# Batch 1's feed-forward work in units of 256 tokens, batch 2's casts later, and second layers held back in batch 0

## The chip, the cores and the metric

The kernel runs on one core of one Trainium2 chip. A core has five engines with queues of their own, each worked in order: TensorE for matrix products (PE in the profile, its weight loads PEld), VectorE (DVE), ScalarE (ACT), GpSimd (POOL) and SyncE (SP), which here issues most of the DMAs. Engines wait for each other by semaphores. Matrix products are written to PSUM, of which this kernel uses eight banks, and copied from there by ACT or DVE. The metric is the device time of one execution in microseconds (us).

## The reference

Two layers, one after the other. The first is causal attention in a sliding window with a bias that falls with distance (batch 8, 8 heads, 576 tokens, head size 64):

```
scores = scale * q @ k.T                       # window of 128, causal
scores = where(0 <= i - j < 128, scores - slope[h] * |i - j|, -1e9)
x = softmax(scores) @ v                        # 4608 tokens x 512 (heads side by side)
```

The second sends every token through eight experts (512 to 1024 to 512), weighted by a matrix P that is normalised over rows and columns eight times:

```
P = exp(x @ w_gate - max);  8 times: rows to sum 1, columns to sum 1, times N/E
out = sum over e of P[:, e] * (relu(x @ w1[e]) @ w2[e])
```

## The kernel before

The program order is written out by hand; each engine runs its instructions in that order. It has three stages: attention, with the products of experts 0 and 1 put between its steps as filling for PE; the normalisation of P, filled in the same way; and experts 2 to 7 with fewer and smaller products. The change lies in the first stage.

Attention goes through 8 batches. A batch of 576 tokens has five key blocks (four of 128, a tail of 64), and every block two halves of four heads: ten half-blocks, counted by `at = 2 * kb + u`. A half-block has scores on PE (`scores`, L372, into `psS`, a pair of two-bank buffers), the exponential on ACT (`exps`, L390), the masking product on DVE (`masks`, L403) and the product with the values on PE (`values`, L426, into `psN`). DVE divides by the row sums (L436, L437, into `xsb`). `turn_x` turns a block of the result: for batches 0, 1, 2 and 7 by PE into `psX` with a copy to `xT` (L457, L465), else by a transposing DMA (L467). `xT` is the input of the experts.

Before a batch's scores, q and k are loaded (`load_qk`, L232, on SP), cast to half precision four times two heads at a time (`cast_qk`: k by ACT at L247, q by DVE at L245, into `c16`), and turned. For batches 0 to 2 `turn_pe` turns them on PE into `psT` (L311); ACT copies the k side to `kN` (L326), DVE the q side to `qN` (L324), and the tail of 64 goes with `j = NDT` through ACT into `tT` (L320). From batch 3 on `turn_qk` issues two transposing DMAs (L261), and `order_qk` copies their result on POOL and DVE (L272). The load of v (L334), its cast on POOL (L344), `load_tail` (L223) and the stores of finished second layers (`store`, L487) are also issued from inside the loop; SP takes all its DMAs in the order written.

`Filler` holds the work of experts 0 and 1 as units of an expert and a span of token blocks of 128. A unit has eight chains of first-layer products (`l1`, L102: four matmuls into one bank `psh`, then a relu on ACT to `hT`, L109) and one second-layer chain for each block (`l2`, L115: eight matmuls into `psy`, then a copy on DVE to `yo`, L499, or to `y_first`, L495). `take` gives the next chain. It starts a unit when no first-layer chain is left and at most two second-layer chains are, takes a second-layer chain after two first-layer ones, and reckons 0.87 us for a first-layer chain of 512 columns and 1.74 us for a second-layer one. `start_unit` takes the first unit in the list whose blocks are written (`ready`) and whose expert is `allowed`; expert 1 is allowed from half-block 4 of batch 1 on. Each half-block takes its share of what is ready: what is left in the list divided by the half-blocks left.

The units are spans of blocks (0, 1), (2, 3), then four blocks each: (4 to 7), (8 to 11) and on. Blocks 0 to 3 are batch 0, 4 to 7 batch 1. Scores, filling, turns, gates and value products share four PSUM banks under the tag `pmm`: all but the scores, which have `psS`.

The loop over half-blocks writes out, in order: budget, the next half-blocks' scores and exponential, 1 us of filling, masks, values, the turn of the finished block, the rest of the filling, and then the loads and casts that are due at this half-block.

Of the kernel before, what the change touches and what calls it, by code (L numbers as in the profile page):

```python
# [14 lines left out]
def kernel(  # L15
# [25 lines left out]
    NG = Ntok // GT  # L41
# [105 lines left out]
    class Filler:  # L147


        def __init__(self, units):  # L150
            self.todo = list(units)
            self.l1: list = []
            self.l2: list = []
            self.l1_us = 0.0
            self.since = 0
            self.ready = 0
            self.allowed = {0}

        def start_unit(self):
            for n, (e, b0, nb, make) in enumerate(self.todo):  # L160
                if b0 + nb <= self.ready and e in self.allowed:
                    self.todo.pop(n)
                    self.l1_us = L1_US * nb / 4
                    self.l1, self.next_l2 = make()
                    return True
            return False

        def take(self):
            if not self.l1 and len(self.l2) <= 2:
                if self.start_unit():  # L170
                    self.since = 0
            use_l2 = bool(self.l2) and (not self.l1 or self.since >= 2)
            if use_l2:
                self.l2.pop(0)()
                self.since = 0
                cost = L2_US
            elif self.l1:
                self.l1.pop(0)()
                self.since += 1
                cost = self.l1_us  # L180
                if not self.l1:
                    self.l2 = self.l2 + self.next_l2
            else:
                return 0.0
            return cost
# [17 lines left out]
    if True:  # L203
# [33 lines left out]
        def cast_qk(b, j):  # L237

            if j == 0:
                c16s[b] = per.tile([P, 2, RI, H, Dh], FP16, name=f"c16_{b}", tag="a8", bufs=8)  # L240
            for n in (1, 0):
                src = raw[b][n][:, 2 * j : 2 * j + 2, :].rearrange("p h (i d) -> p i h d", i=RI)
                to = c16s[b][:, n, :, 2 * j : 2 * j + 2, :]
                if n == 0:
                    nc.vector.tensor_copy(out=to, in_=src)  # L245
                else:
                    nc.scalar.copy(out=to, in_=src)  # L247
            if j == NDT - 1:
                raw.pop(b)
# [52 lines left out]
        def turn_pe(b, kq, j):  # L302

            wide = j == NDT
            ps = aps.tile([P, RI, P], FP32 if wide else FP16, name=f"psT_{b}_{kq}_{j}", tag="pmm", bufs=4)
            for i in range(RI):
                if wide:
                    src = tails[b][:, 2 * i : 2 * i + 2, :]
                else:
                    src = c16s[b][:, kq, i, 2 * j : 2 * j + 2, :]  # L310
                nc.tensor.matmul(  # L311
                    out=ps[:, i, :],
                    lhsT=src.rearrange("p h d -> p (h d)"),
                    rhs=ident32 if wide else ident,
                    is_transpose=True,
                    start=(i == 0),
                    stop=(i == RI - 1),
                )
            if wide:
                nc.scalar.copy(out=QKT[b][2], in_=ps)  # L320
                return
            to = QKT[b][kq][:, j].rearrange("p (r i) -> p r i", i=RI)
            if kq == 0:
                nc.vector.tensor_copy(out=to, in_=ps.rearrange("p i r -> p r i"))  # L324
            else:
                nc.scalar.copy(out=to, in_=ps.rearrange("p i r -> p r i"))  # L326
# [71 lines left out]
        def masks(b, kb, u):  # L398
            nk, nn = sizes(kb)
            pt = pts[b, kb, u]  # L400
            hs = slice(4 * u, 4 * u + 4)
            w = nk + nn
            nc.vector.tensor_tensor(  # L403
                out=pt[0:nk, :, 0:w], in0=pt[0:nk, :, 0:w], in1=mask[0:nk, hs, 0:w], op=ALU.mult
            )
# [38 lines left out]
        def by_pe(b):  # L444
            return b < XPE or b == B - 1
# [53 lines left out]
            nc.vector.tensor_copy(out=yo, in_=ps)  # L499
            stores.append((e, blk, yo))  # L500

        spans = [(0, 2), (2, 2)] + [(4 * g, 4) for g in range(1, NG)]
        order = [(0, 0), (0, 1)]
        for n in range(2, len(spans)):
            order += [(0, n), (1, n - 2)]
        order += [(1, len(spans) - 2), (1, len(spans) - 1)]
        filler = Filler(
            (e, *spans[n], lambda e=e, n=n: unit_atoms(e, *spans[n], aps, ("pmm", "pmm"), (4, 4), keep))
            for e, n in order
        )  # L510
# [77 lines left out]
        def some(n):  # L588
            for _ in range(min(n, len(todo))):
                todo.pop(0)()  # L590
# [36 lines left out]
        for n, (b, kb, u) in enumerate(steps):  # L627
            nxt = steps[n + 1] if n + 1 < len(steps) else None
            at = 2 * kb + u
            left = ((8 if b < XPE else 10) - at) % 10 + 1  # L630
            budget = filler.backlog() / (11 if (b, at) == (XPE, 0) else left)
            if nxt:
                if nxt[0] < XPE and nxt[1:] == (RI - 2, 1):
                    turn_pe(nxt[0], 0, NDT)
                if nxt == (1, 0, 0):
                    cast_qk(1, 0)
                    cast_qk(1, 1)
                    for j in range(NDT):
                        turn_pe(1, 1, j)
                        turn_pe(1, 0, j)  # L640
                        if j < 2:
                            cast_qk(1, j + 2)
                        filler.fill(1.0)
                if n == 0:
                    scores(*nxt)
                elif nxt[2] == 0:
                    scores(*nxt)
                    scores(*nxt[:2], 1)
                exps(*nxt)
            got = filler.fill(1.0)  # L650
            if nxt:
                masks(*nxt)
            values(b, kb, u)
            if n > 0 and u == 0 and by_pe(steps[n - 1][0]):
                turn_x(*steps[n - 1][:2])
            if u == 1 and n // 2 + NKB < B * NKB:
                cast_v(n // 2 + NKB)
            filler.fill(budget - got)
            if at == 0 and b > XPE:
                filler.ready = 4 * b  # L660
            if at < 8 and b < XPE:
                filler.ready = 4 * b + at // 2
            if at == 8 and b < XPE:
                filler.ready = 4 * b + 4
            if u == 1 and not by_pe(b):
                turn_x(b, kb)
            if u == 1:
                if kb == 1 and b > 0:
                    gates(4 * b - 4, 4 * b)
                if n // 2 + NKB + 1 < B * NKB:  # L670
                    load_v(n // 2 + NKB + 1)
            if b == 0 and at == 1:
                load_weights(1)
            if b == 1 and at == 4:
                filler.allowed.add(1)
                nc.sync.dma_start(out=ysp[0, 0:RI].rearrange("m p d -> p m d"), in_=first_y[0])
            if (b, at) == (0, 3):
                load_qk(2)
            if (b, at) == (0, 7):
                homes(1)  # L680
            if (b, at) == (1, 3):
                homes(2)
            if b == 1 and 3 <= at <= 6:
                cast_qk(2, at - 3)
            if b == 1 and 4 <= at <= 7:
                turn_pe(2, 1, at - 4)
                turn_pe(2, 0, at - 4)
            if 1 <= b < B - 2 and at == 3:
                load_qk(b + 2)
            if 1 <= b < B - 2 and at >= 8:  # L690
                cast_qk(b + 2, at - 8)
            if 2 <= b < B - 1:
                if at < 2:
                    cast_qk(b + 1, at + 2)
                if at == 1:
                    turn_qk(b + 1)
                    order_qk(b + 1, 1, range(NDT))
                if at == 5:
                    turn_tail(b + 1)
                if at in (6, 7):  # L700
                    order_qk(b + 1, 0, range(2 * at - 12, 2 * at - 10))
            if b < B - 1 and at == (1 if b > 1 else 5) and b:
                load_tail(b + 1)
            if 10 * b + at >= 66:
                i = 10 * b + at - 66
                if i % 8 == 0:
                    home_last(2 + i // 8)
                (load_w2 if i % 8 < 4 else load_w1)(2 + i // 8, i % 4, 4)
            if (b, at) == (7, 0):
                todo += sums_of(2, *extras(2))  # L710
            if b == 7 and at >= 5:
                some(1)
# [270 lines left out]
        for n in range(N):  # L983
            g = units[n - 1][0]
# [62 lines left out]
```

## Time and profile before

| | |
|---|---|
| median of 3 runs | 1061.02 us (1057.84 to 1062.36) |
| the profiled execution | 1060.31 us, its span 1058.5 us |
| PE busy | 1031.1 us, 97% of the span |
| DVE, ACT, POOL busy | 631.7, 434.5, 77.4 us |
| PE busy in the stretch 0 to 27 us | 17.09 us |
| in 27 to 58 us | 22.19 of 31 us |
| in 58 to 78 us | 19.40 of 20 us |
| in 78 to 113 us | 34.57 of 35 us |

All times within the profile are counted from the span's start. A row of the timeline gives start, length, engine, line, operation, what it writes and reads, and how many instructions in a row are taken together; in brackets, how long the engine stood idle before and what released it. Batch 1's scores begin at 42 us, batch 2's at 76.74, batch 3's at 112.85. An engine's length of one instruction holds a latency that overlaps the next one, so that starts are closer together than lengths.

### The profile page before, as it was taken

What the parts mean: (1) busy time and instruction counts of PE and PEld (TensorE: products, weight loads), DVE (VectorE), ACT (ScalarE), POOL (GpSimd) and SP (SyncE); (2) the same over time, 40 slices, a digit from 0 to 9 for tenths busy, and PEclk for the clock granted to TensorE, in tenths of its full rate; (3) what the DMA queues carried; (4) which work ended last, traced back from release to release, by engine and by line L of the source; (5) the groups of instructions that cost most, each with busy time, mean ns of one, the idle gap of its engine ahead of it and who ended that gap; (6) DMA issues with size and microseconds to landing.
All of it is one profiled execution on the core that took longest, in us unless ns stands there. A gap on an engine that the chain in (4) does not pass through costs nothing.

```text
span 1058.5 us, 21148 instructions
## 1 busy us (share of the span) xinstructions
PE 1031.1 (97%) x9006; PEld 802.9 (76%) x9006; DVE 631.7 (60%) x1171; ACT 434.5 (41%) x729; POOL 77.4 (7%) x139
## 2 busy tenths in 40 slices
PE   6789999999999999999999999999999999999998
PEld 4455444444544888888888888888888888888887
DVE  4655665655687665655655655655655655555555
ACT  6556555555233333333333333333333333333332
POOL 2112032325100000000000000000000000000000
PEclk9999999999999999999999999999999999999999
DMA  9985599879992501211211210211220220220240
GB/s 226 252 221 139 114 201 218 196 154 177 182 207 70 115 23 49 71 26 46 71 39 33 70 49 23 71 39 32 71 65 7 71 68 3 71 71 1 71 90 20
DMA packets 166110, 98.55 MB, mean 93 GB/s; under 512 B 84960, under 2 KB 157440, under 8 KB 166016
## 3 DMA queue, kind: packets, MB, share of 16 engines
q1 hardware_dynamic: 151280, 79.21, 29.4%
q0 software_dynamic: 14304, 17.84, 10.2%
q8 instruction: 70, 1.15, 0.4%
q14 instruction: 24, 0.20, 0.1%
q10 hardware_dynamic: 432, 0.16, 0.1%
HBM read 87.74 MB, written 19.02 MB: 101 GB/s over the span
## 4 chain that ended last, share of the span: by engine, by line
PE 92%; DMA 4%; SPq 2%; DVE 1%; ACT 1%; issue 0%; POOL 0%; ACTq 0%
PE psh L834 36%; PE psS_m L889 31%; PE psh L102 11%; PE psy L115 10%; DMA v<-in_v_dram 2%; DMA k<-in_k_dram 2%; PE psN L426 1%; PE psS L372 1%; DMA xT<-xsb 1%; SPq L334 1%; SPq L223 0%; SPq L288 0%; PE psy L954 0%; PE psG L473 0%; ACT hT L109 0%
## 5 line engine op out<-in xcount | busy, mean ns | idle before, releaser
L841 ACT ACTIVATE hs<-psh 128x512 f16<-128x512 f32 x432 | 258.0, 597 | 453.2 <-PE psh L834 373.7
L834 PE MATMUL psh<-aux,w1l 128*128 128x256 f16 x2880 | 372.6, 273 | 0.2 <-ACT hs L841 0.2
L834 PEld LDWEIGHTS <-w1l 128*128 128x128 f16 x2880 | 281.7, 98 | 33.3 <-issue 0.5
L889 PEld LDWEIGHTS <-hs 128*128 128x128 f16 x2568 | 251.3, 98 | 29.1
L846 DVE TENSOR_TENSOR hs<-hs 128x1024 f16<-128x1024 f16 x107 | 74.1, 693 | 274.5 <-ACT hs L841 274.3
L889 PE MATMUL psS_m<-w2l,hs 128*128 128x256 f16 x1440 | 186.6, 273 | 0.0
L102 PE MATMUL psh<-xT,w1t 128*128 128x512 f16 (+1 forms) x640 | 141.1, 359 | 4.4 <-DMA xT<-xsb 1.7
L115 PE MATMUL psy<-w2t,hT 128*128 128x512 f16 x576 | 133.8, 379 | 3.4 <-DMA w2t<-in_moe_w_dram 2.8
L818 DVE TENSOR_TENSOR aux<-xT,pbc 128x1024 f16<-128x1024 f16 x108 | 131.4, 1217 | 2.5 <-DMA pbc<-ptd 2.5
L109 ACT ACTIVATE hT<-psh 128x512 f16<-128x512 f32 (+1 forms) x160 | 87.6, 556 | 100.6 <-PE psh L102 99.3
L115 PEld LDWEIGHTS <-hT 128*128 128x128 f16 x576 | 53.7, 98 | 64.6 <-issue 4.8
L102 PEld LDWEIGHTS <-w1t 128*128 128x128 f16 x640 | 57.9, 99 | 53.6 <-issue 6.4
L390 ACT ACTIVATE pt<-psS 128x1024 f16<-128x1024 f32 (+2 forms) x80 | 67.5, 852 | 45.9 <-PE psS L372 37.0
L935 DVE TENSOR_TENSOR acc<-acc,psS_m 128x256 f32<-128x256 f32 (+1 forms) x162 | 74.3, 504 | 12.4 <-PE psS_m L889 11.1
L499 DVE CAST yo<-psy 128x512 f16<-128x512 f32 x68 | 46.9, 690 | 55.5 <-PE psy L115 54.3
L403 DVE TENSOR_TENSOR pt<-pt,mask 128x1024 f16<-128x1024 f16 (+2 forms) x80 | 50.2, 627 | 41.5 <-ACT pt L390 41.4
L889 PE MATMUL psS_m<-more,hs 128*128 128x256 f16 x576 | 74.6, 273 | 0.0
L834 PE MATMUL psh<-aux,w1t 128*128 128x256 f16 x576 | 74.6, 273 | 0.0
L849 DVE TENSOR_TENSOR hs<-hs 128x1024 f16<-128x1024 f16 x107 | 73.2, 684 | 0.0
L834 PEld LDWEIGHTS <-w1t 128*128 128x128 f16 x576 | 56.4, 98 | 6.5
L535 POOL DMA_DIRECT2D w2t<-in_moe_w_dram x2 | 1.8, 878 | 705.2 <-PE psS_m L889 669.8
L426 PEld LDWEIGHTS <-pt 128*128 128x128 f16 (+2 forms) x576 | 28.6, 101 | 26.1 <-DVE pt L403 6.8
(83 smaller groups left out, 657.2 us busy)
## 6 DMA issues: line engine op xcount, KB each, us to landing
pbc<-ptd SPq DMA_DIRECT2D x108, 128.0 KB, 4.5
y<-ysp SPq DMA_DIRECT2D x36, 256.0 KB, 4.7
ysp<-yo SPq DMA_DIRECT2D x68, 128.0 KB, 3.1
v<-in_v_dram SPq DMA_DIRECT2D x32, 256.0 KB, 3.9
out_dram<-acc SPq DMA_DIRECT2D x31, 256.0 KB, 2.4
q<-in_q_dram SPq DMA_DIRECT2D x7, 1024.0 KB, 6.4
k<-in_k_dram SPq DMA_DIRECT2D x7, 1024.0 KB, 9.8
w2t<-in_moe_w_dram POOLq DMA_DIRECT2D x4, 1024.0 KB, 14.7
```

Of the source, the lines that this page charges most:

```text
L102: nc.tensor.matmul(out=ps[:, 0:nt], lhsT=w1ts[e][:, dt, P * ft : P * ft + P], rhs=xT[:, b0 : b0 + nb, dt, :], start=(dt == 0), stop=(dt == ...
L109: nc.scalar.activation(out=st["hT"][:, ft, 0:nt], in_=ps[:, 0:nt], func=AF.Relu)
L115: nc.tensor.matmul(out=ps, lhsT=st["hT"][:, ft, P * ms : P * ms + P], rhs=w2ts[e][:, ft, :], start=(ft == 0), stop=(ft == NFT - 1),)
L390: nc.scalar.activation(out=pt[0:nk, :, 0 : nk + nn], in_=ps[0:nk, :, :, 0 : nk + nn].rearrange("p a y n -> p (a y) n"), func=AF.Exp, scale ...
L403: nc.vector.tensor_tensor(out=pt[0:nk, :, 0:w], in0=pt[0:nk, :, 0:w], in1=mask[0:nk, hs, 0:w], op=ALU.mult)
L818: nc.vector.tensor_tensor(out=xs(n).rearrange("p (d b t) -> p d b t", d=NDT, b=2), in0=xT[:, 2 * g : 2 * g + 2].rearrange("p b d t -> p d ...
L834: nc.tensor.matmul(out=ps[:, f, :], lhsT=W1L[e][:, dt, P * ft : P * ft + P], rhs=xs(n)[:, HB * dt : HB * dt + HB], start=(dt == 0), stop=( ...
L841: nc.scalar.activation(out=h[n][:, 2 * i : 2 * i + 2, :], in_=ps, func=AF.Relu)
L846: nc.vector.tensor_tensor(out=t[:, NFT : NFT + NF2, :], in0=a[:, 0:NF2, :], in1=a[:, NF2:NFT, :], op=ALU.add)
L849: nc.vector.tensor_tensor(out=t[:, NFT + NF2 : 2 * NFT, :].rearrange("p f n -> p (f n)").rearrange("p (f t) -> p f t", t=P), in0=a[:, :, P ...
L889: nc.tensor.matmul(out=Ms[g, bank][:, half, :], lhsT=left(n, m, f), rhs=W2L[e][RIGHT[m]][:, f, :], start=(e == 2 and f == 0 and half == 0) ...
L935: nc.vector.tensor_tensor(out=a, in0=a, in1=p2, op=op)
```

## The change

Three things are altered in the writing order of the first stage.

- The spans of batch 1 are of two blocks, like batch 0's: (4, 5) and (6, 7) take the place of (4 to 7), for expert 0 and expert 1. The order of the list stays: expert 0's span n ahead of expert 1's span n - 2.
- `Filler` has a flag `hold`, with which `take` gives no second-layer chain. It is lifted at half-block 7 of batch 0, behind that half-block's filling.
- Batch 2's casts, which stood at half-blocks 3, 4, 5 and 6 of batch 1 (two heads each, k and q), stand at 5 (two of the four), 6 and 7. Its turns on PE, at 4, 5, 6 and 7 before, stand at 6 (two of the four), 7 and 8, in each half-block ahead of the cast.

In the order that results, PE takes expert 0's unit on blocks 4 and 5 ahead of expert 1's first unit, and expert 1's unit on blocks 4 and 5 is also taken within batch 1; the units on blocks 6 and 7 fall into batch 2. From batch 3's scores on PE's order of work is as before. The lines below are moved by at most four in the changed file.

```diff
             self.allowed = {0}
+            self.hold = True
...
-            use_l2 = bool(self.l2) and (not self.l1 or self.since >= 2)
+            use_l2 = bool(self.l2) and not self.hold and (not self.l1 or self.since >= 2)
...
-        spans = [(0, 2), (2, 2)] + [(4 * g, 4) for g in range(1, NG)]
+        spans = [(2 * g, 2) for g in range(4)] + [(4 * g, 4) for g in range(2, NG)]
...
                 filler.ready = 4 * b + 4
+            if (b, at) == (0, 7):
+                filler.hold = False
...
-            if b == 1 and 3 <= at <= 6:
-                cast_qk(2, at - 3)
-            if b == 1 and 4 <= at <= 7:
-                turn_pe(2, 1, at - 4)
-                turn_pe(2, 0, at - 4)
+            if b == 1 and 5 <= at <= 8:
+                for j in ((), (0, 1), (2,), (3,))[at - 5]:
+                    turn_pe(2, 1, j)
+                    turn_pe(2, 0, j)
+                for j in ((0, 1), (2,), (3,), ())[at - 5]:
+                    cast_qk(2, j)
```

## The prediction

> **What bounds the kernel now.** I read the page's busy shares and slices first, then the list of who waited for whom on PE, then PE's and ACT's timelines over the first 160 us, then SP's. Times below are us from the span's start.
>
> ```profile
> PE 1031.1 (97%) x9006; PEld 802.9 (76%) x9006; DVE 631.7 (60%) x1171; ACT 434.5 (41%) x729; POOL 77.4 (7%) x139
> ...
> PE   6789999999999999999999999999999999999998
> ```
>
> PE is busy 97% of the span, so the end moves by what PE loses or wins idle: 27.4 us in all, 18 of them before 58 us. The waits, longest first in total:
>
> ```profile
> PE psT L311 <- ACT c L247: 7.0, 3, 5.3
> ...
> PE psX L457 <- ACT tT L320: 2.9, 1, 2.9
> PE psy L115 <- DMA w2t<-in_moe_w_dram: 2.8, 1, 2.8
> PE psh L102 <- DMA xT<-xsb: 1.7, 1, 1.7
> ...
> PE psh L102 <- ACT hT L109: 0.9, 2, 0.4
> ```
>
> The 7.0 is mostly the cold start, which the change leaves alone. The two waits it aims at are the 2.9 and the 2.8. On PE's timeline (start, length, instructions, and in brackets the idle before and its releaser):
>
> ```profile
> 30.32 1.89 PE L115 MATMUL psy<-w2t,hT 128*128 128x512 f16 x8 [2.75 <-DMA w2t<-in_moe_w_dram]
> ...
> 55.77 0.59 PE L457 MATMUL psX<-ident,xsb 128*128 128x128 f16 x4 [2.89 <-ACT tT L320]
> ...
> 57.89 1.62 PE L102 MATMUL psh<-xT,w1t 128*128 128x256 f16 x8
> ```
>
> The 2.89 is ACT's doing. The turn of block 1 of batch 1 needs the PSUM bank that held batch 1's tail, ACT empties that bank with the copy tT, and tT stands behind batch 2's first k cast, which waits for its load:
>
> ```profile
> 54.62 0.62 ACT L247 CAST c<-k 128x512 f16<-128x512 f32 x1 [2.90 <-DMA k<-in_k_dram]
> 55.14 0.58 ACT L320 CAST tT<-psT 128x512 f16<-128x512 f32 x1
> ...
> 108.94 0.60 ACT L247 CAST c<-k 128x512 f16<-128x512 f32 x1
> ...
> 147.33 0.62 ACT L247 CAST c<-k 128x512 f16<-128x512 f32 x1 [5.18 <-DMA k<-in_k_dram]
> ```
>
> The idle also costs clock. Windows of 1 us; the granted clock is the number before the last two:
>
> ```profile
> 54.00:55.00 1.00, 0.00 (x0) 0.00 (x0) 0.00 (x0) 0.39 (x1) 0.00 (x0) 1.00 1.17 196
> 56.00:57.00 1.00, 1.00 (x12) 0.94 (x9) 0.32 (x1) 1.00 (x2) 0.00 (x0) 0.50 1.21 209
> 58.00:59.00 1.00, 1.00 (x6) 0.69 (x6) 1.00 (x3) 0.50 (x1) 0.00 (x0) 0.50 0.72 120
> 60.00:61.00 1.00, 1.00 (x11) 0.90 (x10) 0.99 (x2) 0.72 (x2) 0.92 (x5) 1.00 0.81 182
> ```
>
> Half speed lasted from about 55.8 to 59.05. The 2.75 idle at 27.6 did not bring it on.
>
> **Part 1, the hold.** Expert 0's first second-layer chain moves behind one group of value products (0.24 us). It still waits for w2t, which lands at 30.3 whatever PE does, so PE resumes at 30.32 as before. It then runs the same work and stands at about 34.8 before batch 1's first k cast (ACT, 35.17, released by its load). That load covers the 0.24: no gain. If it came early, 0.24 would be won. The reordering gives the next first-layer chain another bank, one that doesn't wait for the copy kN ending at 36.86: I take 0.3, between 0 and 0.6.
>
> **Part 2, batch 2's casts later.** ACT reaches tT at 52.1 instead of 55.14. The turn then waits for xsb (DVE, done 52.98) and starts at 53.05. Scores of block 3 follow by 54.2. The first filler chain is now expert 0 on the first 256 tokens of batch 1, which needs the xT copy behind that turn. DVE has queued ahead of it mask 0.69, reciprocal 0.17, product 0.42, from ACT's exponential ending at 53.65, so xT is there at 55.3. Filler starts at 55.33 instead of 57.89: 2.56 won. The clock stays full, so the first two chains take 0.94 instead of 1.46: 0.52 won. The wait of 0.60 at 64.83 (a bank behind a relu) has no counterpart in the new order: 0.60 won. Batch 2's first eight transposes, run inside those 2.56 us before, come later: 0.45 lost. Two relu waits of 0.2 appear where six or eight 256-column chains stand in a row and ACT has two casts and an exponential between them: 0.4 lost. With part 1's 0.3 that is 3.1 won up to batch 2's scores.
>
> **Part 3, units of 256 tokens.** PE pays nothing: 8 matmuls of 256 columns and 4 of 512 both take 0.87 us start to start (59.59 to 62.21 is three times eight; 85.75 to 86.61 is four). ACT pays:
>
> ```profile
> L109 ACT ACTIVATE hT<-psh 128x512 f16<-128x512 f32 x26 | 15.3, 599 | 11.0 <-PE psh L102 11.0
> L109 ACT ACTIVATE hT<-psh 128x256 f16<-128x256 f32 x32 | 12.0, 387 | 7.9 <-PE psh L102 7.0
> ```
>
> Sixteen relus of 512 become 32 of 256: 32 x 0.387 - 16 x 0.599 = 2.8 us more on ACT, hidden while PE has other work. 13.88 us of PE work (16 chains of 0.435, 4 of 1.73) move from batch 2 into batch 1. So batch 2's scores, at 76.74 before, start at 76.74 + 13.88 - 3.1 = 87.5.
>
> Batch 2 is then short of PE cover at its start. ACT has, start to start as its timeline spaces them, kN 0.49, three casts of batch 3 (0.51 each), three exponentials (0.92 each) and a relu of 0.36 for every 0.435 us of PE work. By that queue PE idles 0.5 (the last q copy stands behind two yo casts on DVE), 1.2 and 0.4, against 0.43 before: 1.7 lost. Batch 3's scores start at 87.5 + (112.85 - 76.74 - 13.88) + 1.7 = 111.4 instead of 112.85. The gain is down to 1.45.
>
> **Part 4, what is late next.** SP works in order, and the load of batch 4's q and k stands behind the two transposing DMAs of batch 3, which wait for batch 3's last cast:
>
> ```profile
> 89.59 5.05 SPq L261 DMA_TRANSPOSE qk<-c  x2
> ...
> 99.07 1.13 SPq L232 DMA_DIRECT2D k<-in_k_dram  x1
> ```
>
> ```profile
> k<-in_k_dram SPq DMA_DIRECT2D x1, 1024.0 KB, 9.4
> ```
>
> Transposes to k issue: 9.48. Issue to landing: 9.4. In between stand the same issues after as before. In the run before, k landed at about 108.5 and ACT cast it at 108.94, with no slack to speak of. After, batch 3's last cast ends about 9.35 us behind the start of batch 2's scores (12.85 before; less filler precedes it): ACT's queue to its third exponential is 0.49 + 3 x 0.51 + 3 x 0.92 + 6 x 0.36 = 6.94 with 0.8 of waits for PE, and DVE follows with mask 0.69, reciprocal, product and q cast, 1.6. That is 96.85. So k lands at 96.85 + 18.9 = 115.75, against a step that wants it near 108.5. Behind that cast ACT has batch 3's first exponential and the relus. PE fills four banks and stands: the fourth chain of batch 3 starts at 115.75 + cast 0.5 + exponential 0.92 + relu 0.6 = 117.85 (117.13 before), after 2.2 us idle; the sixth, behind another cast and exponential, at 120.75 (119.90 before). From there the order is the old one. **Sum: +0.85, call it +0.9**: 2.56 + 0.52 + 0.60 + 0.3 - 0.45 - 0.4 - 1.7 = 1.45 won, and 2.3 taken back by the load.
>
> The profiled execution took 1060.31 (span 1058.5), 0.7 under the median of 1061.02; its sum is 1061.2, and on the median 1061.9.
>
> What the trace can't show is bounded so. The new idle of 2.2 lies between one of 1.70 (at 152.93) and one of 2.75, and the clock stayed at 1.00 behind both, so I take 0; if it acts like the 2.89, half of 3.25 us is lost at worst, 1.6. Load times of 8.6 to 10.0 in the batches behind it move the sum by 0.8 either way; 17.45, as batch 2's k needed beside the weights, is the far end.
>
> The Trainium skill, "TensorE: Matmul & The Clock Gate", section "What's actually happening", has the clock halve only after an idle window of some 3.4 us. This trace disagrees: 2.89 us were enough. By the page the new idle costs nothing (1061.9); by the row at 2.89 up to 1.6 (1063.5).
>
> **Rivals.**
> - *The load is no limit* (0.25). For it: transposes or load a little quicker, or batch 3's cast earlier, and k is there. Against it: it would have to gain 2 to 3 us on a chain whose parts all come from rows. The gain of 1.45 stays, or up to 3.1 if batch 2's ACT waits don't show: 1057.9 to 1059.6.
> - *Slower for good* (0.16). Place: the k load of batch 4, ACT's queue behind it. If it takes 17.45 like batch 2's, 8 us are added: 1070. It decides from 4.4 us of further lateness (5.3 less 0.9). For it: ACT already waited 5.18 for the same load one batch later, at 147.33. Against: DMA is idle from 80 to 88 us, the weights are long in.
> - *Faster by over 0.5%* (0.08). All 3.1 stay and the 0.25 and 1.70 waits at 150 to 153 go as well, with the 0.43: 5.5 won, 1055.5. Nothing in the order touches those two.
> - *The hold does nothing*: certain as far as w2t goes; it is in the forecast.
>
> **How the numbers follow.** The forecast (the load takes the gain back, 1060.5 to 1063.5) has 0.51. Half a percent, about what a measurement can tell from no change here, is 5.3 us. Forecast and first rival lie within it: 0.76; slower 0.16; faster 0.08. Range 1057 to 1066: the first rival's end below, the clock's 1.6 and half of what the load could add above.
>
> **What would show it.** Right: no wait of psX for tT near 53; filler from about 55.3; the clock at 1.00 from 55 to 60; batch 2's scores near 87.5; new waits of psh for relus at 91 to 97; the transposing DMAs near 97; ACT waiting some 6 to 7 us for k before 116, and PE idle some 2 us just after. Wrong, if ACT's cast at batch 3's start waits for nothing, or if that wait exceeds 11 us.

## The result, and the profile after

The changed kernel took 1064.99 us (median of 8 runs, 1063.92 to 1065.95) against 1059.70 of the kernel before in the same session (8 runs, 1056.66 to 1062.36). The ratio is 1.0045, with a 95% interval of 1.0032 to 1.0059: 0.45% slower, where 1061.9 us was forecast. The profiled execution took 1064.4 us, its span 1062.6, 4.1 more than before.

The first lines of the page of the changed kernel, its busy shares and two rows of slices:

```profile
PE 1037.3 (98%) x9070; PEld 812.1 (76%) x9070; DVE 632.8 (60%) x1171; ACT 436.5 (41%) x745; POOL 77.8 (7%) x139
...
PE   5899899999999999999999999999999999999998
...
PEclk9989999999999999999999999999999999999999
```

PE's busy time grew by 6.2 us (1031.1 before), although the products are the same. Most of that is work at a lower clock, which the third slice of the clock row shows; some 1.0 us more is busy time at full clock in batch 2 (see part 3 below). PE's timeline shows the places of the steps (start, length, instructions, idle before and its releaser):

```profile
53.16 0.59 PE L458 MATMUL psX<-ident,xsb 128*128 128x128 f16 x4 [0.23 <-ACT tT L321]
...
55.70 1.86 PE L102 MATMUL psh<-xT,w1t 128*128 128x256 f16 x8 [1.11 <-DVE xT L466]
...
115.71 0.31 PE L427 MATMUL psN<-v,pt 64*64 64x65 f16 x4 [1.36 <-DVE pt L404]
...
118.33 1.46 PE L102 MATMUL psh<-xT,w1t 128*128 128x512 f16 x4 [0.78 <-DVE xT L466]
...
125.78 1.02 PE L102 MATMUL psh<-xT,w1t 128*128 128x512 f16 x4 [0.42 <-ACT hT L109]
```

The 2.89 us wait of psX for tT is down to 0.23, and the first chain on batch 1's tokens starts at 55.70 instead of 57.89. But from there to the next start its first two chains take 1.66 us (57.36), where 0.94 was expected. The third line, a wait of the last value products for a mask on DVE, is new.

What PE waited for in batch 2 and at batch 3's start, first in the kernel before (76 to 120 us), then in the changed one (88 to 127 us); columns are the total, the number and the longest:

```profile
PE psh L102 <- ACT hT L109: 0.9, 2, 0.4
PE psh L102 <- DVE xT L465: 0.5, 1, 0.5
```

```profile
PE psh L102 <- ACT hT L109: 1.4, 2, 1.0
PE psN L427 <- DVE pt L404: 1.4, 1, 1.4
PE psh L102 <- DVE xT L466: 0.8, 1, 0.8
PE psS L373 <- ACT c L248: 0.5, 1, 0.5
PE psN L427 <- DVE xsb L438: 0.4, 1, 0.4
```

The table splits the first stage at points that all kernels have: batch 1's first scores, batch 2's, batch 3's, the sixth chain of batch 3 (after the second relu wait), and batch 7's first scores. Columns are the differences of the start times; from there to the end the order is the same in all. So that columns compare, 13.88 us of filling that the change moves from batch 2 into batch 1 are booked in batch 2 throughout (6.94 in E7 and E11, where half of it is moved). E1 to E12 are the experiments below; "half speed" lists the stretches between 40 us and the last 2 us with a granted clock of 0.50. Each row is one profiled execution, and that can lie off the median: E2's and E12's were the slowest of their runs, E5's the fastest. Two things lie outside the sum. Batch 1's first scores come at 41.1 to 42.1 us in most traces, but at 43.2 to 43.6 in E4, E9, E10 and E12. And behind batch 7's first scores all take 811.4 to 812.7 us, but E11 takes 815.1.

| kernel | batch 1 | batch 2 | to 6th chain | to batch 7 | sum | median us | half speed |
|---|---|---|---|---|---|---|---|
| before | 34.75 | 36.11 | 7.05 | 127.23 | 205.14 | 1059.70 | 55.7-59.1 |
| changed | 34.73 | 40.05 | 9.30 | 125.35 | 209.43 | 1064.99 | 50.5-60.7, 118.8-122.2 |
| E1 casts only | 32.54 | 36.78 | 7.05 | 125.27 | 201.64 | 1059.23 | 50.0-53.4 |
| E2 units only | 36.27 | 39.36 | 10.31 | 126.38 | 212.32 | 1064.18 | 49.7-53.1, 56.5-63.3, 117.9-124.8 |
| E3 old units | 32.53 | 36.78 | 7.74 | 125.48 | 202.53 | 1057.91 | 50.0-53.4 |
| E4 | 32.03 | 40.08 | 9.31 | 126.15 | 207.57 | 1064.83 | 117.6-121.0 |
| E5 early k | 31.61 | 40.43 | 10.05 | 124.89 | 206.98 | 1065.44 | 113.6-120.4 |
| E6 q on ACT | 34.69 | 39.16 | 7.94 | 124.61 | 206.40 | 1063.32 | 50.0-60.2 |
| E7 filling kept | 34.41 | 38.32 | 7.93 | 125.64 | 206.30 | 1061.97 | 50.0-60.2 |
| E8 | 32.53 | 36.79 | 7.10 | 128.35 | 204.77 | 1059.53 | 49.3-52.8 |
| E9 spare | 31.61 | 40.04 | 10.16 | 125.87 | 207.68 | 1063.92 | 116.2-119.6 |
| E10 old units, spare | 31.31 | 36.78 | 7.36 | 127.04 | 202.49 | 1056.84 | none |
| E11 kept, spare | 31.29 | 38.31 | 7.58 | 125.76 | 202.94 | 1059.09 | 356.5-359.9 |
| E12 all | 31.63 | 39.36 | 7.00 | 126.16 | 204.15 | 1058.94 | none |

The changed kernel loses nothing in batch 1 and gains nothing there either. It loses 3.9 in batch 2 and 2.25 behind it, and 1.9 comes back later, where a wait of 0.68 (137.93) of before is down to 0.25 and one of 1.70 (152.93) is gone.

### The profile page after: what moved, and what is told of

Read it like the earlier page. It is cut to its first block, busy times and chain, and to the rows that moved or that the text cites. A ratio compares the mean times of both kernels' runs of the same rounds, so it can differ in the third digit from the quotient of the medians.

```text
span 1062.6 us, 21293 instructions
## 1 busy us (share of the span) xinstructions
PE 1037.3 (98%) x9070; PEld 812.1 (76%) x9070; DVE 632.8 (60%) x1171; ACT 436.5 (41%) x745; POOL 77.8 (7%) x139
## 4 chain that ended last, share of the span: by engine, by line
PE 85%; DVE 0%; ACT 0%; issue 0%
PE psh L838 36%; PE psS_m L893 31%; PE psy L115 8%; PE psh L102 8%; PE psN L427 1%; PE psS L373 1%; PE psy L958 0%; PE psG L474 0%; DVE yo L500 0%; PE psX L458 0%; PE psC L763 0%; DVE pt L404 0%; ACT hs L845 0%; PE psP L778 0%; DVE L_sb L766 0%; PE psS L380 0%
## 5 line engine op out<-in xcount | busy, mean ns | idle before, releaser
L102 PE MATMUL psh<-xT,w1t 128*128 128x512 f16 (+1 forms) x704 | 146.1, 350 | 4.8 <-DVE xT L466 3.1
L109 ACT ACTIVATE hT<-psh 128x512 f16<-128x512 f32 (+1 forms) x176 | 89.8, 522 | 105.8 <-PE psh L102 104.2
L102 PEld LDWEIGHTS <-w1t 128*128 128x128 f16 x704 | 66.0, 101 | 52.9 <-issue 9.6
L838 PEld LDWEIGHTS <-w1t 128*128 128x128 f16 x576 | 56.4, 98 | 6.5
```

The lines of the kernel that those rows point to most:

```text
L102: nc.tensor.matmul(out=ps[:, 0:nt], lhsT=w1ts[e][:, dt, P * ft : P * ft + P], rhs=xT[:, b0 : b0 + nb, dt, :], start=(dt == 0), stop=(dt == ...
L109: nc.scalar.activation(out=st["hT"][:, ft, 0:nt], in_=ps[:, 0:nt], func=AF.Relu)
L838: nc.tensor.matmul(out=ps[:, f, :], lhsT=W1L[e][:, dt, P * ft : P * ft + P], rhs=xs(n)[:, HB * dt : HB * dt + HB], start=(dt == 0), stop=( ...
```

## The experiments

Two theories stood at first. CLOCK: the changed kernel's batch 1 runs at half speed for 10 us, and that costs the time. COVER: the filling that left batch 2 hid ACT's and DVE's queues and the load of batch 4's k, and these now show. Each session had its own runs of the kernel before: 1059.23 us for E1 to E4 (23 runs), 1059.22 for E5 to E8 (25) and 1059.64 for E9 to E12 (29).

**E1, the casts alone** (kernel before, only the block of batch 2's casts and turns changed).

```diff
-            if b == 1 and 3 <= at <= 6:
-                cast_qk(2, at - 3)
...
+            if b == 1 and 5 <= at <= 8:
```

> The kernel before with the third part alone: batch 2's casts and turns at the later half-blocks, units and second layers as before. Theory COVER (the loss comes from filling that left batch 2, so that its ACT and DVE queues and the load of batch 4's k show): no filling moves here, so the stall of 2.9 us behind tT goes and little is given back: 2 to 3 us faster than before, a ratio of 0.997 to 0.998, and ACT's first cast of batch 4 waits less than 1 us. Theory CLOCK (the loss comes from PE's clock being halved from about 50.4 to 60.4 us in the changed kernel, against 55.8 to 59.05 before): the half-speed stretch starts near 50 here as well, and the ratio is 1.000 to 1.003.

1059.23 us (12 runs), ratio 0.9998 [0.9986, 1.0009]. The profiled execution is 3.5 shorter up to batch 7; the median moved by nothing. The ratio lies between the two theories' ranges. The runs lie between 1056.5 and 1062.0, so a gain of some 2 us can't be told here. The casts are not what costs.

**E2, the units alone** (kernel before, only the spans changed).

```diff
-        spans = [(0, 2), (2, 2)] + [(4 * g, 4) for g in range(1, NG)]
+        spans = [(2 * g, 2) for g in range(4)] + [(4 * g, 4) for g in range(2, NG)]
```

> The kernel before with the first part alone: units of 256 tokens in batch 1. Theory COVER: batch 2 takes about 26 us from its first scores to batch 3's, as in the changed kernel (22.2 before, with the moved work taken off), ACT waits 3 us or more for batch 4's k, and the ratio is 1.003 to 1.006 or more, since the stall behind tT stays. Theory CLOCK: the half-speed stretch is the 3.3 us of before, and the ratio is 1.000 to 1.002.

1064.18 us (6 runs), ratio 1.0051 [1.0034, 1.0068], in COVER's range. The whole loss comes with the units of 256 tokens. CLOCK isn't refuted by it: its condition was a half-speed stretch of 3.3 us, and the trace has 17 us of them behind 40 us.

**E3, hold and casts with the old units** (the changed kernel without its line on spans).

> The changed kernel with the old units of 512 tokens in batch 1: hold and later casts stay. Theory COVER: like the casts alone, a ratio of 0.996 to 0.998. Theory CLOCK: 1.000 to 1.003, with half speed from about 50 us on, since half-blocks 0 to 4 of batch 1 run as in the changed kernel. The hold itself is expected at 0 to 0.5 us by both.

1057.91 us (11 runs), ratio 0.999 [0.9982, 0.9999]. That too is between the two ranges. With E1 this leaves nothing in the times that could be put down to the hold.

**E4, PE kept busy in batch 1.** Eight matmuls of 512 columns that nobody reads, two ahead of the value products of each of half-blocks 1 to 4.

```diff
+            if (b, 2 * kb + u) in ((1, 1), (1, 2), (1, 3), (1, 4)):
+                for _ in range(2):
+                    nc.tensor.matmul(out=psN, lhsT=ident, rhs=mask[:, 0:2, :].rearrange("p a n -> p (a n)"), start=True, stop=True)
```

> The changed kernel with two more matmuls of 512 columns ahead of the value products of half-blocks 1 to 4 of batch 1, into the same bank, which the value products then overwrite: work whose result nobody reads, 8 x 0.216 us, put where PE waits for the masks. Theory CLOCK: the clock stays at 1.00 past 50 us or drops for at most 3.5 us, batch 2's first scores come at 87 to 88.5 instead of 90.3, and the time falls by 2 to 3 us against the changed kernel: a ratio to before of about 1.002. Theory COVER: what is won there is given back behind the load of batch 4's k; the time stays within 0.5 us of the changed kernel, a ratio of 1.004 to 1.006.

1064.83 us (5 runs), ratio 1.0049 [1.0037, 1.0062]. The half speed at 50 to 60 went, and batch 1 became 2.7 shorter in the trace; the median stayed, as COVER had it. I read this as CLOCK falling. E7 and E11 showed later that this was too much: the clock costs. The trace also shows where part of the gain went: its clock fell earlier instead, from 32.3 to 35.7, and batch 1's first scores came 1.6 later (43.34 against 41.70).

**E5, batch 4's k loaded earlier**, at half-block 0 of batch 2, ahead of batch 3's transposing DMAs.

```diff
-            if 1 <= b < B - 2 and at == 3:
+            if 1 <= b < B - 2 and at == (0 if b == 2 else 3):
```

> The changed kernel, with the load of batch 4's q and k issued at half-block 0 of batch 2 instead of half-block 3, so ahead of batch 3's transposing DMAs in SP's queue. LOAD (the late load of batch 4's k is what costs): ACT's cast of it waits for nothing, where the changed kernel waited 3.55 us at 118.04; the sixth chain of batch 3 starts near 122 instead of 125.78, and the time is 1061 to 1063. DVE (the queue at the end of batch 2 costs, the load stands in its shadow): the cast waits for nothing either, but batch 3's scores stay at 116.5, the sixth chain comes within 1 us of 125.8, and the time is 1064 to 1065.5. I lean to LOAD for about half of the loss: 1062.5.

1065.44 us (6 runs), ratio 1.0062 [1.0043, 1.0081]: no gain, so LOAD alone falls. The time is in DVE's range, but batch 3's scores came at 113.67 and the sixth chain at 123.72, neither as DVE had them. ACT's wait for k before batch 3's first exponential is gone, but PE's wait for DVE's mask is 1.79 us instead of 1.36, and PE ran at half speed from 113.6 to 120.4.

**E6, batch 3's copies of the turned q on ACT.**

```diff
-                (nc.vector, nc.gpsimd)[n].tensor_copy(
+                copy = nc.scalar.copy if (b, n) == (3, 0) else (nc.vector, nc.gpsimd)[n].tensor_copy
+                copy(
```

> The changed kernel, with batch 3's two copies of the turned q made by ACT instead of DVE. DVE: the wait of 1.36 us of psN for DVE at 115.7 goes, batch 3's scores start near 114.5 to 115 instead of 116.48, and 1.5 to 2 us stay won at the end: 1062.5 to 1063.5. LOAD: the scores start as early, but ACT's wait for batch 4's k grows from 3.55 us by what was won, the sixth chain stays at 125.8, and the time at 1064 to 1065.

1063.32 us (7 runs), ratio 1.0036 [1.0021, 1.0051]. DVE's timeline in the changed kernel shows what was in the way:

```profile
113.64 1.22 DVE L273 COPY qN<-qk 128x512 f16<-128x512 f16 x2
114.78 0.68 DVE L500 CAST yo<-psy 128x512 f16<-128x512 f32 x1
115.38 0.27 DVE L404 TENSOR_TENSOR pt<-pt,mask 64x256 f16<-64x256 f16 x1
...
116.12 1.09 DVE L273 COPY qN<-qk 128x512 f16<-128x512 f16 x2
```

The mask that PE waits for until 115.71 stands behind two q copies and a yo cast. Without the copies, PE's wait there and ACT's wait for k are

```profile
114.58 0.31 PE L428 MATMUL psN<-v,pt 64*64 64x65 f16 x4 [0.49 <-DVE pt L405]
```

```profile
118.32 0.62 ACT L248 CAST c<-k 128x512 f16<-128x512 f32 x1 [3.71 <-DMA k<-in_k_dram]
```

The first is down from 1.36, the second hardly up from 3.55. Batch 2 is 0.9 shorter, and the time 1.7 by the medians (1.0 by the ratios), as DVE had it; batch 3's scores came at 115.35, just behind its 114.5 to 115. The interval overlaps that of the changed kernel, so the size isn't settled.

**E7, half of the filling returned to batch 2.** Expert 1's unit on blocks 4 and 5 isn't begun before blocks 6 and 7 are written (the same condition also stands in the sum of what is ready).

```diff
-                if b0 + nb <= self.ready and e in self.allowed:
+                if b0 + nb <= self.ready and e in self.allowed and ((e, b0) != (1, 4) or self.ready >= 8):
```

> The changed kernel, with expert 1's unit on blocks 4 and 5 not begun before blocks 6 and 7 are written: 6.95 us of filling (8 chains of 0.435 and 2 of 1.73) go back from batch 1 into batch 2, and the units stay at 256 tokens. COVER (what costs is the filling that left batch 2, through ACT's and DVE's queues and the load): batch 2's scores start near 83.4, batch 2 takes some 30 us and batch 3's scores start at 113 to 114.5; the wait for batch 4's k falls under 1.5 us; the time is 1059 to 1061.5. SIZE (the units of 256 tokens cost by themselves, by ACT's shorter and more numerous relus): the time stays at 1063.5 to 1065.

1061.97 us (12 runs), ratio 1.0029 [1.0011, 1.0047]: between the two, 0.5 above COVER's range. The units are still of 256 tokens, and 3.0 us came back by the medians, 1.7 by the ratios. In the trace batch 3's scores came at 113.87, as COVER had them, and ACT's wait for batch 4's k was 1.87, a little over its 1.5. The runs spread from 1056.5 to 1066.5. The two whose mean granted clock was 1.000 took 1056.54 and 1056.55; the three at 0.992 took 1063.95 to 1066.49. That was the reason to look at the clock again.

**E8, earlier loads with the old units**, from batch 4's on.

```diff
-            if 1 <= b < B - 2 and at == 3:
+            if 1 <= b < B - 2 and at == (3 if b == 1 else 0):
```

> The hold and the later casts with the old units of four blocks, and the loads of q and k of batches 4 and on issued at half-block 0 of the batch two before instead of half-block 3. LOAD as a cost of the kernel before too: the casts of batch 5's k, which waited 3.98 us at 145 without this edit, wait for nothing, and 0.5 to 2 us are won against 1057.9 of the same kernel with late loads: 1056 to 1057.5. If ACT's wait for k is covered there by what PE has banked, nothing changes: 1057.5 to 1058.5.

1059.53 us (12 runs), ratio 1.0007 [0.9994, 1.0019]: not faster, and above both ranges. ACT's wait for batch 5's k went, but the stretch up to batch 7 grew by 2.9 against E3. The load stands ahead of the transposing DMAs now. The pair at 156.93 took 9.59 us, and PE waits soon behind:

```profile
156.93 9.59 SPq L262 DMA_TRANSPOSE qk<-c  x2
```

```profile
171.89 2.76 PE L102 MATMUL psh<-xT,w1t 128*128 128x512 f16 x12 [1.06 <-DVE xsb L438]
175.10 0.56 PE L427 MATMUL psN<-v,pt 128*64 128x65 f16 x8 [0.44 <-DVE xsb L438]
...
210.21 0.55 PE L427 MATMUL psN<-v,pt 128*64 128x65 f16 x8 [1.03 <-DVE xsb L438]
```

The next pair took 9.46; the others here and in E3 took 4.5 to 6.2. That the longer transposes cause these waits was not tested.

**E9, spare matmuls in PE's waits.** They are not read by anything. The first argument names chains by expert, first block and number.

```diff
+    def spare(ps, n):
+        for _ in range(n):
+            nc.tensor.matmul(out=ps, lhsT=ident, rhs=mask[:, 0:2, :].rearrange("p a n -> p (a n)"), start=True, stop=True)
...
+            spare(ps, {(0, 4, 0): 4, (0, 8, 0): 3}.get((e, b0, ft), 0))
...
+            spare(ps, 4 if (e, blk) == (0, 0) else 0)
...
+            spare(psN, {(1, 1): 2, (1, 2): 4, (2, 9): 4}.get((b, 2 * kb + u), 0))
```

> The changed kernel, with matmuls that nobody reads put into TensorE's waits, each group shorter than the wait that the trace shows there: 4 of 512 columns (0.86 us) ahead of the first second-layer chain, 2 and 4 ahead of the value products of half-blocks 1 and 2 of batch 1 (waits of 0.60 and 1.02), 4 ahead of the first chain on batch 1's tokens (1.11), 4 ahead of the last value products of batch 2 (1.36) and 3 ahead of the first chain of batch 3 (0.78). The output is the same. In the earlier traces the clock falls and rises on a grid of 3.41 us, after a stretch in which TensorE was busy some 60% or less. CLOCK (half speed at 50 to 60 and near 118 costs the time): TensorE stays at full speed from 45 us on in most runs, batch 2's scores start at 87.1 (as in the trace of the kernel with the earlier load, where the clock was full) instead of 90.31, the sixth chain of batch 3 near 122, and the time is 1060 to 1061.5. COVER (what the late queues of ACT and DVE at batch 3's start cost is there at any clock): batch 2's scores come at 87.1 as well, but what is won goes into longer waits, and the time is 1063.5 to 1065.

1063.92 us (6 runs), ratio 1.0042 [1.0027, 1.0058]. The half speed at 50 to 60 is gone in the trace and batch 1 takes 31.61 us, but one group stands in the wrong place: the wait of 1.36 belongs to the half-block before the last, so the four matmuls ahead of the last one's products stand outside any wait, and half speed still came at 116.2:

```profile
114.08 0.31 PE L434 MATMUL psN<-v,pt 64*64 64x65 f16 x4 [1.35 <-DVE pt L410]
...
118.55 1.54 PE L93 MATMUL psN<-mask,ident 128*128 128x512 f16 x4
```

The time is in COVER's range, but CLOCK's condition of full speed from 45 us on wasn't met, so the trace doesn't decide between the theories.

**E10, spare matmuls with the old units** (E3 with 4; 2 and 4; and 4 ahead of batch 3's first chain).

> Hold and later casts with the old units, and spare matmuls in its waits: 4, then 2 and 4 as in the run above, and 4 ahead of the first chain of batch 3 (wait of 1.19). CLOCK: the half speed at 50 to 53.4 goes, the scatter of 1057.1 to 1060.4 becomes smaller, and the median falls from 1057.9 by up to 1.7: 1056.2 to 1057.5. If the clock is hidden here (this kernel's runs at full clock were no faster than those below it): 1057.5 to 1058.5. The distance to the run above is what the 256-token units cost at the same clock: 3 to 4 us by CLOCK and COVER together, 6 or more by COVER alone.

1056.84 us (12 runs), ratio 0.9976 [0.9964, 0.9988]. This beats both kernels: 2.8 us under the kernel before. Seven of its twelve runs had a mean clock of 1.000. It is in CLOCK's range. Against E3 it is 1.1 lower, with intervals that overlap a little; the scatter didn't become smaller (4.1 us, 3.2 in E3). E9 lies 7.1 above it, which is the 6 or more that COVER alone was to give, though E9's misplaced group (1.5 us long) is part of that.

**E11, spare matmuls in E7** (4; 2 and 4; 4 ahead of the first chain on batch 1's tokens; 5 ahead of batch 3's).

> The kernel that returned 6.95 us of filling to batch 2, with spare matmuls: 4, then 2 and 4, 4 ahead of the first chain on batch 1's tokens, and 5 ahead of the first chain of batch 3 (wait of 1.37). Its twelve runs lay at 1056.5 where the clock was full all through (2 runs) and at 1059.6 to 1066.5 where it was not. CLOCK: all runs come to the first group, median 1056 to 1057.5. COVER alone: the median stays at 1061 to 1062.5.

1059.09 us (12 runs), ratio 1.0 [0.9988, 1.0012], 2.9 under E7, with intervals that barely touch. CLOCK's range ended 1.6 below it and COVER's began 1.9 above; the spread shrank from 10 to 5.8 us. This trace alone has a wait of 2.2 us (for DVE, at 354.3) and half speed behind it (356.5 to 359.9), far behind the stretches of the table.

**E12, the three together** (E5, E6 and spare matmuls).

> The changed kernel with the three suspected costs taken away together: batch 4's k loaded from half-block 0 of batch 2 on, batch 3's copies of the turned q on ACT, and spare matmuls (4; 2 and 4; 4; 1 ahead of the last value products of batch 2; 1 ahead of the first chain of batch 3). If clock, load and DVE's queue are all that it lost: 1056 to 1058.5, as the kernel with the old units. If the 256-token units cost by themselves: 1060 or more.

1058.94 us (12 runs), ratio 0.9994 [0.9985, 1.0003]. That lies 0.4 above the first range and 1.1 below the second. With all three taken away, the changed kernel stands level with the kernel before: the ratio went from 1.0045 to 0.9994, some 5.4 us. Singly they moved it to 1.0036 (E6), 1.0042 (E9) and 1.0062 (E5). ACT's first steps of batch 3 are then free of the wait:

```profile
113.63 0.61 ACT L254 CAST c<-k 128x512 f16<-128x512 f32 x1
115.06 1.02 ACT L398 ACTIVATE pt<-psS 128x1024 f16<-128x1024 f32 x1 [0.83 <-PE psS L380]
```

The cast ends before batch 3's scores come; now it is the exponential that waits for PE. The stretch to the sixth chain is 7.00, that of before. Batch 2 stays at 39.36, 2.6 above the same stretch with the old units (36.78), at a full clock in both. E12 and E10 differ in the units, the k load, the q copies and the places of a few spare matmuls; 2.1 us in the median is what is left there. The spare matmuls also help the old units (E10), so the changed kernel is level only with a kernel before that has none.

## Why the prediction was right or wrong

The change stayed within half a percent, on the slow side, but barely: by the medians the loss is 5.29 us, and the prediction had put half a percent at 5.3. The range of 1057 to 1066 held the time; the 1060.5 to 1063.5 given for the forecast itself did not, and the sum was 3 us short. By the profiled executions, counted from the span's start, as forecast and as measured:

| step | forecast | measured |
|---|---|---|
| up to batch 2's scores (part 1 and 2) | -3.1 | -0.3 |
| batch 2 (part 3) | +1.7 | +3.9 |
| to the sixth chain (part 4) | +2.3 | +2.25 |
| from there to batch 7 | 0 | -1.9 |
| sum | +0.9 | +4.0 |

**Part 2, "the clock stays full": wrong, and the largest miss.** PE's own order came as worked out: filler at 55.70 (55.33 forecast). But the granted clock fell at 50.5, before the idle that the change removes. Stretches of the changed kernel's trace; the first number pair is the stretch and its length, then PE's busy time, and the third number from the end is the clock:

```profile
47.09:50.51 3.42, 1.74 (x28) 0.96 (x25) 3.31 (x11) 2.03 (x3) 0.00 (x0) 1.00 1.12 231
50.51:53.92 3.41, 3.18 (x48) 2.81 (x48) 1.97 (x6) 2.30 (x3) 0.00 (x0) 0.50 1.22 207
53.92:57.33 3.41, 2.30 (x24) 1.68 (x19) 2.01 (x5) 1.31 (x3) 0.00 (x0) 0.50 1.20 206
57.33:60.75 3.42, 3.42 (x24) 2.50 (x22) 0.61 (x2) 1.30 (x4) 1.31 (x4) 0.50 0.80 160
60.75:64.16 3.41, 3.41 (x27) 2.44 (x25) 0.00 (x0) 2.15 (x6) 1.98 (x6) 1.00 1.01 282
...
115.36:118.78 3.42, 2.15 (x19) 1.07 (x20) 3.18 (x11) 0.74 (x2) 0.00 (x0) 1.00 1.29 218
118.78:122.19 3.41, 3.41 (x16) 1.32 (x15) 1.62 (x4) 1.40 (x2) 1.32 (x4) 0.50 0.83 221
```

In the stretch ahead of each fall PE was busy 1.74 and 2.15 of 3.4 us, in pieces, with no wait over 1.36 us. The clock came back only behind a stretch in which PE was busy all through. Where the clock was full, batch 1 came out close to the forecast: 45.49 us from its first scores to batch 2's, in E5's trace and in E9's, which has spare matmuls in the waits (31.61 in the table, with the moved filling). The forecast makes it 45.8 (87.5 less 41.7, the start that part 1 gives). So the terms 2.56, 0.52, 0.60, 0.45 and 0.4 held as a sum at full clock; whether each of them held was not tested. What failed is the assumption on the clock, worth 3.1 us (48.61 in the changed kernel's trace). The time bound of 1.6 for the clock was put at batch 3's start, where it was about right, and not at batch 1, where it was needed.

**Part 3, the loss of 1.7 in batch 2: right in part, size 3.9.** Of the three new waits of 0.5, 1.2 and 0.4, two are there: 0.50 at the first scores and 0.95 for a relu. The view puts the 0.50 down to a cast on ACT, but the scores read qN, and its copy on DVE, behind two yo casts as forecast, ends at 91.25, just ahead of them. Missed was DVE at the end of batch 2: PE waits 0.43 for it at 109.18, and from 111.36 to 118.6 it is busy without a break, in which PE waits another 1.36. For the end of batch 2 I had followed ACT's queue only. Missed as well was PE itself, which was to pay nothing: of the 3.9, 2.9 is idle time (3.35 against 0.43), and 1.0 is longer busy time at full clock (36.70 against 35.68, the moved filling booked); why was not followed. E6 takes 0.9 of the 3.9 away. Of the rest, 0.67 comes with the later casts at any unit size (36.78 against 36.11 in E1 and E3). Some 2.4 to 2.6 stays with the small units in E6 and E12 (39.16 and 39.36 against 36.78). In E12 the relu wait of 0.95 and the waits of 0.65 and 0.44 for DVE make up 1.6 of it (2.04 less the 0.42 that the old units wait for a relu), and PE's longer busy time 0.8 (36.70 against 35.86 in E10).

**Part 4, the load of batch 4's k: the chain was right, the share not.** SP and ACT in the changed kernel:

```profile
99.90 4.54 SPq L262 DMA_TRANSPOSE qk<-c  x2
...
108.99 1.73 SPq L233 DMA_DIRECT2D k<-in_k_dram  x1
```

```profile
118.04 0.62 ACT L248 CAST c<-k 128x512 f16<-128x512 f32 x1 [3.55 <-DMA k<-in_k_dram]
```

The transposes come 9.6 us behind batch 2's scores (9.35 forecast), the cast 18.1 behind them (18.9 forecast). The 2.25 behind batch 3's scores agree with the forecast's 2.3, but by luck: with the wait for k and a full clock (E6) the stretch is 7.94, without it 7.00 (E12), so the load is worth 0.9. The other 1.3 are shared by half speed at 118.8 and a longer wait for xT on DVE (0.78 against 0.23 in E6); no run separates them. With the load alone taken away (E5), nothing was won. The forecast of an ACT wait of 6 to 7 us was too long: 3.55, since all that precedes came later.

**"Nothing in the order touches those two"** (the waits at 150 to 153, in the rival of a faster kernel): wrong for the larger one. The 0.25 is still there (0.26 at 157.77), but the 1.70 for a transposing DMA is gone, and with the shorter wait at 143.39 it makes the 1.9 us that came back, which hid part of the miss. What in the new order moved it was not followed.

**Part 1, the hold**: batch 1's first scores came at 41.70 instead of 41.99, the 0.3 of the forecast. In the six traces with the hold and without spare matmuls they come at 41.14 to 41.93, in the three without the hold at 41.81 to 42.11; the medians of E1 and E3 can't tell so little apart. w2t was waited for 0.46 instead of 2.75, only since PE, at half speed from 23.2 to 26.6, came later; it resumed at 30.29, as forecast.

**What the loss is, then.** In the median 5.3 us. It comes with the units (E2, E3). E12 takes as much away (5.4) by taking three things together: half speed, DVE's queue at batch 3's start and the late k. Singly none of them brought it back: E6 won 1.0 to 1.7, E5 nothing, and E4, without half speed at 50 to 60, nothing. That they hide each other is argued, not shown, since no two of them were taken away without the third; and 2.1 us against the old units with spare matmuls (E10) stay unexplained.

That the clock has a part of its own is seen best in E7 and E11 (2.9 us). The mean granted clock of the single runs bears on its share in the changed kernel. Among runs of the same kernel and session (198 runs in all), a mean clock lower by 0.001 goes with 0.56 us more (standard error 0.06). The changed kernel's runs average 0.9931, those of the kernel before 0.9964 to 0.9966 by session; by this the clock makes up some 1.9 of the 5.3 us, an estimate from a correlation, in which long waits may also lower the clock. E9 points the same way: its mean clock of 0.9975 is above that of the kernel before, and it still took 4.3 us longer. The kernel before with spare matmuls alone wasn't tried, so how much of E10's 2.8 us is due to the casts stays open.

## What to carry to other kernels

Filling that is moved to an earlier place uncovers the queues at the later one: follow every engine there, not only the one that looked short, and don't expect that removing one wait alone wins its length: here E5 won nothing and E6 1.0 to 1.7 us. A stretch in which TensorE is only half busy in small pieces can cost the clock for the next 3.4 to 10 us; with a few unread matmuls in its waits, batch 1 ran at full speed in all five traces that had them. The runs became steadier in E11, not in E9 or E10. A single trace is weak evidence here: E1's was 3.5 us shorter up to batch 7, and its median not at all.

## What the runs showed of the hardware

In every trace the granted clock changed only on a grid of 3.41 us, whose edges fit within 0.01 us in a run (23.20, 50.51, 60.75, 118.78 and 122.19 in the changed kernel), and the grid lay differently against the kernel from trace to trace: the first edge behind 18 us stood at 18.05 in E5, 19.79 in the changed kernel and 20.59 in E9, though at 19.23 or 19.24 in E1, E3, E6 and E7. So whether a weak stretch fills a step also depends on where the grid lies. E5 is the changed kernel up to about 79 us, with the grid elsewhere; the same work ran at full speed:

```profile
48.77:52.18 3.41, 2.63 (x50) 1.93 (x51) 3.04 (x9) 1.60 (x3) 0.00 (x0) 1.00 1.17 212
52.18:55.59 3.41, 2.06 (x33) 1.56 (x34) 2.53 (x7) 1.91 (x3) 0.00 (x0) 1.00 1.21 196
55.59:59.00 3.41, 3.41 (x39) 3.08 (x37) 0.61 (x2) 2.81 (x8) 0.87 (x3) 1.00 1.27 226
```

Between 18 and 130 us, every fall in these traces followed a step in which PE was busy 63% or less; but steps of 43% (before, from 28.4) and 60% (E5, above) were not followed by one, so the busy share alone is not the criterion. At half speed, steps of 97% or more always brought the clock back; of the thirteen between 67 and 93% two did (85%, in E8 and in E12). The Trainium skill, "TensorE: Matmul & The Clock Gate", section "What's actually happening", has an activity window of some 3.4 us that runs freely and isn't reset when a kernel starts; the grid agrees (3.41 us). The same section of the Trainium skill has the clock halve after an idle window. This case's traces disagree: in the changed kernel it halved after windows that were 46, 51 and 63% busy, with no wait over 1.36 us in them.
